# Gated linear attention and two MLPs: the scores of a chunk only within its halves, the first half handed to the second through the state

## The chip, the cores and the metric

One core of a Trainium2 chip. The time is the device time of one launch in microseconds (us), the median of three runs. TensorE (PE in the rows) multiplies matrices, VectorE (DVE), ScalarE (ACT) and GpSimd (POOL) work element by element, and SyncE (SP) issues the DMAs.

## The reference

Attention runs per head over 4 batches of 8 heads, 768 tokens, 48 features, and two MLPs follow:

```python
state = np.zeros((B, H, D, D)); y = np.zeros_like(q)
for t in range(S):
    state = alpha[:, :, t, :, None] * state + np.einsum('bhd,bhe->bhde', k[:, :, t], v[:, :, t])
    y[:, :, t] = np.einsum('bhd,bhde->bhe', q[:, :, t], state)
x = y.transpose(0, 2, 1, 3).reshape(B * S, H * D)   # 3072 tokens x 384
h = x @ w_in;  g = h * sigmoid(1.702 * h);  x = g @ w_out      # 384 -> 2048 -> 384
h = x @ w2_in; g = h - tanh(h);             out = g @ w2_out
```

The decay alpha is one number per token and feature, between 0.8 and 1.

## The kernel before

**Attention in chunks.** The 3072 tokens are cut into 24 chunks of 128, six to a sequence. All eight heads of a chunk are worked on together as four pairs: the features of a pair's first head lie on partitions 0 to 47, those of its second on 64 to 111. A chunk goes like this. Its decays are loaded twice, once reversed in time (L229), and two scans on VectorE (L237) turn them into running products; k and q are multiplied by these (`a_scale`), so that the decay between any two tokens of a chunk is a product of two factors. `a_scores` multiplies k with q: the keys are the stationary operand, 128 of them on 128 columns of the array, and 176 columns stream, 128 queries and then an identity of 48 that `eye` has written behind them, which gives k transposed for later. The two heads of a pair use the two row halves of the array. Call this group S (L273). It is done in two calls of two pairs each, x = 0 and x = 1. The scores leave PSUM under a causal mask: for the first eight chunks ScalarE copies and GpSimd cuts the triangle (L278, L283), for the others VectorE multiplies by a stored mask (L280, four instructions of 128x256 a chunk). ScalarE copies the transposed keys (L286).

`a_out` has three groups. Y (L302) multiplies the state that the earlier chunks left with q, 48 rows and 128 columns; the first chunk of a sequence has none. I (L305) multiplies the values with the masked scores, 128 rows and 128 columns, onto the same sums. D (L312) multiplies transposed keys with values, which is what the chunk adds to the state; the last chunk of a sequence has none. VectorE then adds it (L316) and multiplies by the decay of the chunk (L317). All of it is fp32, which the array does in two passes, and the trace counts each pass: eight matmuls are "x16".

`a_evac` copies the sums to SBUF (L326), sends them to DRAM and reads them back in the layout of the MLP (L331, L332), casts them to a high part (L333) and subtracts it to get a low part (L334).

**MLPs.** Each runs in six blocks of 512 tokens (j) and sixteen steps of 128 hidden units (m), 192 steps in all. A step has nine matmuls of 128x512 into the hidden layer (L343) and, three steps later, nine out of it (L350): three products of high and low parts for each of three pieces of the model dimension. Call these the MLP matmuls; there are 3456. Their activations and splits are on ScalarE, VectorE and GpSimd.

**Order.** The first four chunks come before the first MLP step, with the weights of the first MLP being converted on VectorE beside them (`conv`: L160, L161, L173, L191). The other twenty are spread over the steps of layer 1's first five blocks: `attend(g, r)`, r = 0 to 3, is called after the first matmuls of some steps. At r = 0 stand the first scan of the next chunk and the scores x = 0, at r = 1 the scores x = 1 and the second scan, at r = 2 `a_out` and the scaling of the next chunk, at r = 3 the evacuation and the loads of the chunk after the next. A scheduler that runs a model of the machine then decides the order of each engine's instructions, so groups are moved and broken up by it. DMAs are issued in order by SyncE.

Of the kernel before, what the change touches and what calls it, by code (L numbers as in the profile page):

```python
# [17 lines left out]
C = 128  # L18
# [13 lines left out]
CE = C + D  # L32
QW = 2 * AW + NP * C + NP * CE
# [35 lines left out]
def linear_attention_mlps(ctx, tc, xq, xv, fa, fv, cst, w1, w2, out):  # L69
# [13 lines left out]
    wt = [T(f"wt{i}", (128, WC), mybir.dt.int16) for i in range(2)]  # L83
# [16 lines left out]
    AR = 7184  # L100
# [15 lines left out]
    COLS = (AW, AW, NP * CE, NP * C, VW)  # L116
# [9 lines left out]
    third = [gt[:, 0:AW], gt[:, AW : 2 * AW], xsf[:, 0 : NP * CE], xsf[:, NP * CE :][:, :NB], gt[:, 2 * AW : 2 * AW + VW]]  # L126
    sm = [carve(4 * C) for _ in range(2)]
    kts = [carve(4 * D) for _ in range(2)]
# [36 lines left out]
    def w_check(l, m):  # L165
        t = wt[m % 2]
# [41 lines left out]

    def qq(g):
        return dec3(g, 2)  # L210
# [4 lines left out]
    def eye(g):  # L215
        for hh in range(2):
            r = slice(64 * hh, 64 * hh + D)
            A.copy(qq(g)[r, :, C:], ident[r, r].unsqueeze(1).to_broadcast([D, NP, D]))
# [4 lines left out]
    def a_load(g):  # L223
# [7 lines left out]
        SP.dma_start(out=qq(g)[:, :, :C], in_=xq[g, :, 2 * AW : 2 * AW + NB].rearrange("p (h t) -> p h t", h=NP))  # L231
# [9 lines left out]
    def a_scale(g):  # L241
        e = V if g < FULL else G
        e.tensor_tensor(out=qkk(g), in0=qkk(g), in1=dec3(g, 0)[:, :, :C], op=ALU.mult)  # L243
        e.tensor_tensor(out=qq(g)[:, :, :C], in0=qq(g)[:, :, :C], in1=dec3(g, 1)[:, :, 1:], op=ALU.mult)
# [21 lines left out]
    def a_scores(g, x, b):  # L266
        u = (2 * g + x) % 2
        q, k = qq(g), qkk(g)
        o = [bank[b + hh][:, : 2 * CE].rearrange("p (a t) -> p a t", a=2) for hh in range(2)]
        for i in range(2):  # L270
            for hh in range(2):
                r = slice(64 * hh, 64 * hh + D)
                P.matmul(out=o[hh][:, i], lhsT=k[r, 2 * x + i], rhs=q[r, 2 * x + i], start=True, stop=True)  # L273
        s4 = sm[u].rearrange("p (b a t) -> p b a t", b=2, a=2)
        kt = kts[u].rearrange("p (b a t) -> p b a t", b=2, a=2)
        for hh in range(2):
            if g < FULL:
                A.copy(s4[:, hh], o[hh][:, :, :C])  # L278
            else:
                V.tensor_tensor(out=s4[:, hh], in0=o[hh][:, :, :C], in1=mask.unsqueeze(1).to_broadcast([128, 2, C]), op=ALU.mult)  # L280
        if g < FULL:
            s3 = sm[u].rearrange("p (a t) -> p a t", a=4)
            G.affine_select(out=s3, in_=s3, pattern=[[0, 4], [1, C]], channel_multiplier=1, base=1 - C,  # L283
# [364 lines left out]
```

## Time and profile before

| | |
|---|---|
| median of three runs | 974.35 us (973.78 to 976.83) |
| the profiled execution | 975.3 us |
| its span | 973.2 us |
| mean granted clock of TensorE | 0.995 |
| TensorE busy | 940.9 us (97%) |
| VectorE, ScalarE, GpSimd busy | 606.0, 460.6, 191.7 us |

The rows below come from that execution; times in them start with its span. A matmul's duration in a row is longer than its share of TensorE's time, because matmuls overlap: what one costs is read from one start to the next. In a timeline row, the time is that of the first of the merged instructions, the duration runs to the end of the last, and the brackets hold the engine's idle time before it and what it waited for. `out<-in` are the program's names, `48*128 48x176` a weight of 48 rows and 128 columns and 48 rows of 176 streamed columns.

### The profile page before, as it was taken

The page shows a single profiled execution, that of the slowest core. Times are in us where ns is not written, and L with a number is a line of the kernel's source. Part 1 is how long each engine was busy: PE and PEld are TensorE (multiplying, and loading weights), DVE is VectorE, ACT ScalarE, POOL GpSimd, SP SyncE. Part 2 cuts the span into 40 slices and gives each one's busy share as a digit, 9 for nine tenths or more (in the row PEclk, how much of TensorE's full clock was granted, in tenths as well). Part 3 has the DMA queues.
Part 4 walks back from the last instruction along what each step waited for, and adds up shares of the span by engine and source line. Part 5 has one row for each costly group of instructions (what it writes and reads, how often), then busy time and mean ns, then how long its engine had stood idle before and what let it go on. Part 6 is the DMA issues. An engine that isn't in the chain of part 4 may idle for free.

```text
span 973.2 us, 13227 instructions
## 1 busy us (share of the span) xinstructions
PE 940.9 (97%) x4870; PEld 739.7 (76%) x4870; DVE 606.0 (62%) x914; ACT 460.6 (47%) x969; POOL 191.7 (20%) x150
## 2 busy tenths in 40 slices
PE   5968999999999999999999999999999999999997
PEld 4646787777777777777788888888888888888885
DVE  7989742442343453453339996766777777766663
ACT  4445434333443534434344555554556656545542
POOL 1222202434434434334230110100100101000000
PEclk9999999999999999999999999999999999999999
DMA  9795221432445463761324330100233420000001
GB/s 282 245 305 166 85 53 28 131 92 67 137 141 153 151 205 116 247 196 41 92 71 158 134 130 1 65 33 0 70 126 98 161 100 0 33 1 1 33 0 37
DMA packets 58043, 101.84 MB, mean 105 GB/s; under 512 B 4992, under 2 KB 37376, under 8 KB 57968
## 3 DMA queue, kind: packets, MB, share of 16 engines
q1 hardware_dynamic: 57968, 100.90, 32.6%
q8 instruction: 40, 0.66, 0.3%
q14 instruction: 35, 0.29, 0.1%
HBM read 86.73 MB, written 14.16 MB: 104 GB/s over the span
## 4 chain that ended last, share of the span: by engine, by line
PE 87%; DMA 5%; DVE 5%; issue 1%; ACT 1%; SPq 0%; POOL 0%; DVEq 0%; ACTq 0%
PE bank L350 40%; PE bank L343 40%; DMA arena<-xq 4%; PE bank L273 3%; PE bank L305 2%; DMA raw<-w 2%; DVE arena L237 1%; PE bank L302 1%; PE bank L312 1%; DVE cf L161 1%; DVE cf L173 1%; DVE wlo L191 0%; DVE cf L160 0%; DVE xs L173 0%; ACT arena L248 0%
## 5 line engine op out<-in xcount | busy, mean ns | idle before, releaser
L343 PE MATMUL bank<-xhi,whi 128*128 128x512 f32 x576 | 230.0, 400 | 0.2 <-ACT xhi L333 0.2
L343 PE MATMUL bank<-xlo,whi 128*128 128x512 f32 x576 | 229.8, 399 | 0.0
L343 PE MATMUL bank<-xhi,wlo 128*128 128x512 f32 x576 | 229.0, 398 | 0.0
L350 PE MATMUL bank<-ghi,whi 128*128 128x512 f32 x576 | 229.0, 398 | 0.0
L350 PE MATMUL bank<-ghi,wlo 128*128 128x512 f32 x576 | 228.5, 397 | 0.0
L350 PE MATMUL bank<-glo,whi 128*128 128x512 f32 x576 | 223.8, 396 | 0.0
L361 ACT CAST ghi<-gt 128x512 fp32r<-128x512 f32 x192 | 119.0, 620 | 199.2 <-DVE gt L373 124.1
L358 DVE SCALAR_TENSOR_TENSOR gt<-gt,bank 128x512 f32<-128x512 f32 x96 | 65.5, 682 | 125.8 <-ACT gt L357 122.7
L362 DVE TENSOR_TENSOR glo<-gt,ghi 128x512 fp32r<-128x512 f32 x128 | 93.2, 728 | 79.4 <-ACT ghi L361 76.0
L343 PEld LDWEIGHTS bank<-xhi,whi 128*128 128x128 f32 x576 | 109.0, 189 | 27.4 <-issue 1.6
L343 PEld LDWEIGHTS bank<-xlo,whi 128*128 128x128 f32 x576 | 109.1, 189 | 26.2 <-issue 1.4
L343 PEld LDWEIGHTS bank<-xhi,wlo 128*128 128x128 f32 x576 | 109.2, 190 | 25.7 <-issue 0.6
L350 PEld LDWEIGHTS bank<-ghi,whi 128*128 128x128 f32 x576 | 108.5, 188 | 26.4 <-issue 1.2
L350 PEld LDWEIGHTS bank<-ghi,wlo 128*128 128x128 f32 x576 | 108.5, 188 | 25.4 <-issue 0.8
L350 PEld LDWEIGHTS bank<-glo,whi 128*128 128x128 f32 x576 | 108.3, 188 | 25.1 <-DVE arena L243 0.2
L362 POOL TENSOR_TENSOR glo<-gt,ghi 128x512 fp32r<-128x512 f32 x64 | 85.8, 1341 | 139.0 <-ACT ghi L361 127.8
L410 POOL TENSOR_TENSOR xlo<-arena,xhi 128x512 fp32r<-128x512 f32 x18 | 27.9, 1574 | 307.6 <-ACT xhi L409 307.6
L357 ACT ACTIVATE gt<-bank 128x512 f32<-128x512 f32 x96 | 57.1, 595 | 64.0 <-PE bank L343 63.1
L237 DVE TENSOR_TENSOR_SCAN arena<-arena,seg 112x516 f32<-112x516 f32 x46 | 62.8, 1365 | 35.4 <-DMA arena<-xq 34.7
L371 DVE SCALAR_TENSOR_TENSOR arena<-arena,bank 128x512 f32<-128x512 f32 x96 | 65.7, 685 | 30.4 <-ACT arena L369 29.7
L369 ACT ACTIVATE arena<-bank 128x512 f32<-128x512 f32 x96 | 57.3, 597 | 42.2 <-PE bank L343 41.9
L373 DVE SCALAR_TENSOR_TENSOR gt<-arena 128x512 f32<-128x512 f32 x96 | 68.3, 711 | 9.4
(85 smaller groups left out, 853.7 us busy)
## 6 DMA issues: line engine op xcount, KB each, us to landing
raw<-w SPq DMA_DIRECT2D x64, 768.0 KB, 4.7
arena<-xq SPq DMA_DIRECT2D x46, 224.0 KB, 3.0
arena<-xq SPq DMA_DIRECT2D x22, 451.5 KB, 5.8
xt<-arena SPq DMA_DIRECT2D x96, 48.0 KB, 3.0
xlo<-xt SPq DMA_DIRECT2D x24, 192.0 KB, 4.1
x1t<-xs SPq DMA_DIRECT2D x6, 768.0 KB, 5.2
arena<-x1t SPq DMA_DIRECT2D x6, 768.0 KB, 4.6
out<-xs SPq DMA_DIRECT2D x18, 256.0 KB, 2.3
```

Of the source, the lines that this page charges most:

```text
L237: V.tensor_tensor_scan(out=dec(g, n), data0=src(g, n), data1=seg, initial=0.0, op0=ALU.mult, op1=ALU.max)
L273: P.matmul(out=o[hh][:, i], lhsT=k[r, 2 * x + i], rhs=q[r, 2 * x + i], start=True, stop=True)
L343: P.matmul(out=h, lhsT=w[m][:, ws], rhs=x[:, k, :n], start=c == 0, stop=c == 3 * KT - 1)
L350: P.matmul(out=acc[k][:, :n], lhsT=w[m][:, ws], rhs=x[s % 3][:, :n], start=m == 0 and c == 0, stop=m == MT - 1 and c == 2)
L357: A.activation(out=th[i][:, :n], in_=h, func=AF.Tanh, scale=0.851)
L358: V.scalar_tensor_tensor(out=gf[i][:, :n], in0=th[i][:, :n], scalar=1.0, in1=h, op0=ALU.add, op1=ALU.mult)
L361: A.copy(ghi[s % 3][:, :n], gf[s % 2][:, :n])
L362: e.tensor_tensor(out=glo[s % 3][:, :n], in0=gf[s % 2][:, :n], in1=ghi[s % 3][:, :n].bitcast(F32), op=ALU.subtract)
L369: A.activation(out=u, in_=h, func=AF.Square, accum_out=usum[:, s - NS1 :][:, :1])
L371: V.scalar_tensor_tensor(out=p, in0=u, scalar=P3, in1=h, op0=ALU.mult, op1=ALU.mult)
L373: V.scalar_tensor_tensor(out=gf[i], in0=w, scalar=PD, in1=p, op0=ALU.add, op1=ALU.mult)
L410: G.tensor_tensor(out=xlo[i][:, k], in0=xr[:, k], in1=xhi[i][:, k].bitcast(F32), op=ALU.subtract)
```

## The change

The chunk is treated as two halves of 64 tokens. Keys and values are stored reversed in time, so half u = 1 (partitions 64 to 127) is the first in time.

Scores are computed only within a half: sixteen matmuls of 64 keys, streaming 64 queries and the identity of 48 (112 columns), where there were eight of 128 keys and 176 columns. The two halves go to the two column halves of the array and the two heads to the two row halves, so four such tiles exist. One call makes all four pairs, into two banks. The mask is VectorE's for all chunks, two multiplications of 128x512 whose input is read twice along the queries; the quadrant of the mask that pairs first-half keys with second-half queries is set to zero. GpSimd's and ScalarE's part in the masking is gone. ScalarE copies the transposed keys as before, in two instructions.

`a_out` becomes two functions. `a_half`, at r = 1, makes D of the first half (eight matmuls over 64 keys), all of I (unchanged: 128 keys, with zeros in the quadrant), Y of the first half's queries (64 columns), then VectorE adds the first half's D to the state, or copies it for the first chunk of a sequence, and D of the second half is made. `a_rest`, at r = 2, makes Y of the second half's queries with the state so far, and the state gets the second D and the decay.

The queries are loaded by two DMAs, one a half, with shorter runs, since an identity now stands behind each half. The buffers of the masked scores and the transposed keys hold a whole chunk, once; the check of the second layer's weights has one buffer instead of two.

```diff
-CE = C + D
-QW = 2 * AW + NP * C + NP * CE
+
+C2 = C // 2
+CE = C2 + D
+QW = 2 * AW + NP * C + 2 * NP * CE
...
-    wt = [T(f"wt{i}", (128, WC), mybir.dt.int16) for i in range(2)]
+    wt = [T(f"wt{i}", (128, WC), mybir.dt.int16) for i in range(1)]
...
-    sm = [carve(4 * C) for _ in range(2)]
-    kts = [carve(4 * D) for _ in range(2)]
+    sm = carve(2 * NP * C).rearrange("p (b a t) -> p b a t", b=2, a=NP)
+    kts = carve(2 * NP * D).rearrange("p (b a t) -> p b a t", b=2, a=NP)
...
+    def qx(g):
+        return src(g, 2).rearrange("p (h x t) -> p h x t", h=NP, x=2)
+
     def qq(g):
-        return dec3(g, 2)
+        return qx(g)[:, :, :, :C2]
...
-        SP.dma_start(out=qq(g)[:, :, :C], in_=xq[g, :, 2 * AW : 2 * AW + NB].rearrange("p (h t) -> p h t", h=NP))
+        for x in range(2):
+            SP.dma_start(out=qq(g)[:, :, x], in_=xq[g, :, 2 * AW : 2 * AW + NB].rearrange("p (h x t) -> p h x t", h=NP, x=2)[:, :, x])
...
-    def a_scores(g, x, b):
-        u = (2 * g + x) % 2
-        q, k = qq(g), qkk(g)
-        o = [bank[b + hh][:, : 2 * CE].rearrange("p (a t) -> p a t", a=2) for hh in range(2)]
-        for i in range(2):
+    def a_scores(g, b):
+        q, k = qx(g), qkk(g)
+        o = [bank[b + hh][:, : NP * CE].rearrange("p (a t) -> p a t", a=NP) for hh in range(2)]
+        for p in range(NP):
+            for hh in range(2):
+                for u in range(2):
+                    r, st = slice(64 * hh, 64 * hh + D), slice(C2 * u, C2 * u + C2)
+                    P.matmul(out=o[hh][st, p], lhsT=k[r, p, st], rhs=q[r, p, 1 - u], start=True, stop=True)
+        for hh in range(2):
+            A.copy(kts[:, hh], o[hh][:, :, C2:])
+        for hh in range(2):
+            V.tensor_tensor(out=sm[:, hh].rearrange("p a (x t) -> p a x t", x=2),
+                            in0=o[hh][:, :, :C2].unsqueeze(2).to_broadcast([128, NP, 2, C2]),
+                            in1=mask.rearrange("p (x t) -> p x t", x=2).unsqueeze(1).to_broadcast([128, NP, 2, C2]), op=ALU.mult)
+
+
+    def y_at(b, p, hh, u):
+        return bank[b + hh][64 * (p % 2) : 64 * (p % 2) + D, C * (p // 2) + C2 * (1 - u) :][:, :C2]
+
+    def y_state(g, b, u):
+        for p in range(NP):
             for hh in range(2):
                 r = slice(64 * hh, 64 * hh + D)
...
+                P.matmul(out=y_at(b, p, hh, u), lhsT=state[r, p], rhs=qq(g)[r, p, 1 - u], start=False, stop=not u and p >= 2)
+
+    def deltas(g, u):
+        dl = bank[7][:DP, NP * D * u : NP * D * (u + 1)].rearrange("p (a e) -> p a e", a=NP)
+        st = slice(C2 * u, C2 * u + C2)
+        for p in range(NP):
+            for hh in range(2):
+                P.matmul(out=dl[64 * hh : 64 * hh + D, p], lhsT=kts[st, hh, p], rhs=vt(g)[st, p, D * hh : D * hh + D],
+                         start=True, stop=True)
+        return dl
+
+    def a_half(g, b):
         c = g % NCH
...
+        dl = deltas(g, 1)
+        for p, hh in [(p, hh) for x in range(2) for hh in range(2) for p in (2 * x, 2 * x + 1)]:
+            P.matmul(out=bank[b + hh][64 * (p % 2) : 64 * (p % 2) + D, C * (p // 2) :][:, :C], lhsT=vt(g)[:, p, D * hh : D * hh + D],
+                     rhs=sm[:, hh, p], start=p < 2, stop=False)
         if c:
...
+            y_state(g, b, 1)
+            V.tensor_tensor(out=state, in0=dl, in1=state, op=ALU.add)
+        else:
+            V.tensor_copy(state, dl)
         if c < NCH - 1:
+            deltas(g, 0)
+
+    def a_rest(g, b):
+        y_state(g, b, 0)
+        if g % NCH < NCH - 1:
             dl = bank[7][:DP, : NP * D].rearrange("p (a e) -> p a e", a=NP)
...
+            V.tensor_tensor(out=state, in0=dl, in1=state, op=ALU.add)
+            V.tensor_tensor(out=state, in0=state, in1=dec3(g + 1, 0)[:, :, C:].to_broadcast([DP, NP, D]), op=ALU.mult)
...
-    def attend(g, r, b0=5, b1=5):
+    def attend(g, r, b=5):
         if r == 0:
             prep(g + 1, 0)
-        if r < 2:
-            a_scores(g, r, (b0, b1)[r])
+            a_scores(g, b)
+        if r == 1:
+            a_half(g, b)
         if r == 2:
-            a_out(g, b0)
+            a_rest(g, b)
...
+    V.memset(mask[C2:, C2:], 0.0)
```

How the change moves instructions shows at three places. The first is TensorE in the middle of layer 1 (a chunk's output groups; the names are the lines of each kernel). Before:

```order
L302 MATMUL bank_129<-arena,state 48x128
L302 MATMUL bank_130<-arena,state 48x128
L305 MATMUL bank_129<-arena 48x128 x2
L305 MATMUL bank_130<-arena 48x128 x2
L305 MATMUL bank_129<-arena 48x128 x2
L305 MATMUL bank_130<-arena 48x128 x2
L312 MATMUL bank_131<-arena 48x48 x4
```

And now, where a chunk's middle stands:

```order
L303 MATMUL bank_130<-arena 48x48 x8
L311 MATMUL bank_128<-arena 48x128 x2
L311 MATMUL bank_129<-arena 48x128 x2
L311 MATMUL bank_128<-arena 48x128 x2
L311 MATMUL bank_129<-arena 48x128 x2
L296 MATMUL bank_128<-arena,state 48x64
L296 MATMUL bank_129<-arena,state 48x64
```

Y stood ahead of I and D behind it; now D of the first half leads, I follows, and Y comes last, with D of the second half (not in the piece) behind it.

The second is VectorE in the same stretch of the program, between scores and state: scans (L237, now L243), masks (L280, now L284) and an MLP instruction (L358, now L365). Before:

```order
L358 SCALAR_TENSOR_TENSOR gt<-gt,bank_127 128x512
L237 SCALAR_TENSOR_TENSOR arena<-arena,seg 112x516
L239 RECIPROCAL seg<-arena 112x4
L280 TENSOR_TENSOR arena<-bank_129,cs 128x256
L237 SCALAR_TENSOR_TENSOR arena<-arena,seg 112x516
L236 MEMSET seg 112x4
L280 TENSOR_TENSOR arena<-bank_130,cs 128x256
```

And now:

```order
L243 SCALAR_TENSOR_TENSOR arena<-arena,seg 112x516
L245 RECIPROCAL seg<-arena 112x4
L243 SCALAR_TENSOR_TENSOR arena<-arena,seg 112x516
L242 MEMSET seg 112x4
L284 TENSOR_TENSOR arena<-bank_128,cs 128x512
L284 TENSOR_TENSOR arena<-bank_129,cs 128x512
L365 SCALAR_TENSOR_TENSOR gt<-gt,bank_127 128x512
L315 TENSOR_TENSOR state<-bank_130,state 112x192
```

One pair of masks stood between the two scans of the next chunk and one behind both; now both masks stand behind both scans, and the addition in mid-chunk (L315) follows them.

The third is VectorE before the first MLP matmul, behind the subtraction that makes chunk 2's low part (L334, now L341), with scans and weight conversions of the fourth chunk's time. Before:

```order
L334 TENSOR_TENSOR xlo_106<-xlo_106,xhi_104 128x3x128
L316 TENSOR_TENSOR state<-bank_131,state 112x192
L237 SCALAR_TENSOR_TENSOR arena<-arena,seg 112x516
L191 TENSOR_TENSOR wlo_87<-xs,whi_71 128x768
L173 SCALAR_TENSOR_TENSOR cf_102<-raw_95,cf_102 128x768
L317 TENSOR_TENSOR state<-state,arena 112x192
```

And now:

```order
L341 TENSOR_TENSOR xlo_105<-xlo_105,xhi_103 128x3x128
L243 SCALAR_TENSOR_TENSOR arena<-arena,seg 112x516
L162 TENSOR_SCALAR xs<-raw_97 128x768
L315 TENSOR_TENSOR state<-bank_130,state 112x192
L193 TENSOR_TENSOR wlo_83<-xs,whi_67 128x768
L245 RECIPROCAL seg<-arena 112x4
L249 TENSOR_TENSOR arena<-arena 112x512
L163 SCALAR_TENSOR_TENSOR xs<-raw_97,xs 128x768
L162 TENSOR_SCALAR cf_101<-raw_95 128x768
L243 SCALAR_TENSOR_TENSOR arena<-arena,seg 112x516
L284 TENSOR_TENSOR arena<-bank_128,cs 128x512
L284 TENSOR_TENSOR arena<-bank_129,cs 128x512
L325 TENSOR_TENSOR state<-bank_130,state 112x192
```

Before, the subtraction and then the state's addition (L316) and decay (L317) of a chunk came in close order; now the addition in mid-chunk (L315), two masks (L284) and the addition of the second half (L325) all stand behind that subtraction.

## Rows read from the trace of the kernel before

**Rows 1.** The page, part 1: busy time and share of the span, by engine.

```profile
PE 940.9 (97%) x4870; PEld 739.7 (76%) x4870; DVE 606.0 (62%) x914; ACT 460.6 (47%) x969; POOL 191.7 (20%) x150
```

**Rows 2.** Windows: length; PE, PEld, DVE, ACT, POOL busy (count); clock, DMA share, GB/s.

```profile
0.00:66.00 66.00, 46.83 (x305) 34.84 (x306) 57.79 (x86) 29.66 (x80) 14.20 (x14) 1.00 0.90 275
66.00:112.00 46.00, 41.67 (x212) 29.56 (x211) 44.19 (x66) 22.79 (x50) 10.59 (x6) 0.93 0.52 159
112.00:480.00 368.00, 366.23 (x2262) 281.99 (x2261) 155.09 (x264) 149.94 (x334) 134.24 (x108) 1.00 0.40 122
480.00:966.00 486.00, 486.00 (x2096) 393.33 (x2094) 348.23 (x500) 257.37 (x505) 32.65 (x22) 1.00 0.19 63
```

**Rows 3.** The page, part 4: the chain of waits that ended last, by engine.

```profile
PE 87%; DMA 5%; DVE 5%; issue 1%; ACT 1%; SPq 0%; POOL 0%; DVEq 0%; ACTq 0%
```

**Rows 4.** Timeline of TensorE from its first MLP matmul, waits in brackets.

```profile
65.50 1.03 PE L343 MATMUL bank<-xhi,whi 128*128 128x512 f32 x2 [0.18 <-ACT xhi L333]
...
68.11 0.87 PE L273 MATMUL bank<-arena 48*128 48x176 f32 x8 [1.58 <-ACT whi L190]
...
78.00 0.64 PE L302 MATMUL bank<-arena,state 48*48 48x128 f32 x8 [2.75 <-ACT arena L286]
```

**Rows 5.** Timeline of TensorE, 300 to 309 us: start, duration, operation, number merged.

```profile
300.30 0.40 PE L343 MATMUL bank<-xlo,whi 128*128 128x512 f32 x1
300.63 0.87 PE L273 MATMUL bank<-arena 48*128 48x176 f32 x8
301.43 0.38 PE L312 MATMUL bank<-arena 128*48 128x48 f32 x8
301.75 0.50 PE L343 MATMUL bank<-xhi,wlo 128*128 128x512 f32 x1
302.08 0.40 PE L343 MATMUL bank<-xhi,whi 128*128 128x512 f32 x1
...
306.04 0.40 PE L343 MATMUL bank<-xhi,wlo 128*128 128x512 f32 x1
306.37 0.66 PE L302 MATMUL bank<-arena,state 48*48 48x128 f32 x16
306.95 1.08 PE L305 MATMUL bank<-arena 128*48 128x128 f32 x16
307.87 0.35 PE L312 MATMUL bank<-arena 128*48 128x48 f32 x8
308.14 0.51 PE L343 MATMUL bank<-xhi,whi 128*128 128x512 f32 x1
308.49 0.39 PE L343 MATMUL bank<-xlo,whi 128*128 128x512 f32 x1
```

**Rows 6.** Timeline of TensorE at 347 us: a scores group broken in two.

```profile
347.04 0.86 PE L273 MATMUL bank<-arena 48*128 48x176 f32 x4
347.83 0.51 PE L343 MATMUL bank<-xhi,whi 128*128 128x512 f32 x1
...
348.74 0.86 PE L273 MATMUL bank<-arena 48*128 48x176 f32 x4
```

**Rows 7.** Groups of instructions by line, VectorE: busy us, mean ns, idle before.

```profile
L280 DVE TENSOR_TENSOR arena<-bank,cs 128x256 f32<-128x256 f32 x64 | 24.2, 415 | 18.4 <-PE bank L273 18.3
L316 DVE TENSOR_TENSOR state<-bank,state 112x192 f32<-112x192 f32 x16 | 5.7, 353 | 16.3 <-PE bank L312 16.2
L358 DVE SCALAR_TENSOR_TENSOR gt<-gt,bank 128x512 f32<-128x512 f32 x96 | 65.5, 682 | 125.8 <-ACT gt L357 122.7 <-POOL arena L244 2.8
```

**Rows 8.** The decay loads, line 229, 140 to 480 us: issue to landing.

```profile
DMA to landing us min/median/max: 3.9/6.0/9.6
```

**Rows 9.** Who waited for whom, TensorE, 140 to 480 us: total, times, longest.

```profile
PE bank L302 <- ACT arena L286: 1.4, 2, 0.8
```

**Rows 10.** Timeline of ScalarE at 56 us: cast of chunk 2, copy of chunk 3.

```profile
55.60 0.51 ACT L333 CAST xhi<-xlo 128x384 fp32r<-128x384 f32 x1 [2.51 <-DMA xlo<-xt]
56.02 0.64 ACT L326 COPY arena<-bank 112x256 f32<-112x256 f32 x2
```

More of the change, by code (lines that the diff above doesn't have):

```diff
@@ L217, in eye @@
             r = slice(64 * hh, 64 * hh + D)
-            A.copy(qq(g)[r, :, C:], ident[r, r].unsqueeze(1).to_broadcast([D, NP, D]))
+            A.copy(qx(g)[r, :, :, C2:], ident[r, r].unsqueeze(1).unsqueeze(1).to_broadcast([D, NP, 2, D]))
     def vt(g):
@@ L243, in a_scale @@
         e.tensor_tensor(out=qkk(g), in0=qkk(g), in1=dec3(g, 0)[:, :, :C], op=ALU.mult)
[L244 removed]
+        e.tensor_tensor(out=qq(g), in0=qq(g), in1=dec3(g, 1)[:, :, 1:].rearrange("p h (x t) -> p h x t", x=2), op=ALU.mult)
     def a_guard(g):
@@ L276, in a_scores @@
[L276 to L283, printed above, removed]
-                            compare_op=ALU.is_ge, fill=0.0)
@@ L285, in a_scores @@
-        for hh in range(2):
-            A.copy(kt[:, hh], o[hh][:, :, C:])
-    def a_out(g, b):
-        c = g % NCH
-        q = qq(g)
-        y = [bank[b + hh][:, : 2 * C].rearrange("p (a t) -> p a t", a=2) for hh in range(2)]
-        heads = [(p, hh) for a in range(2) for hh in range(2) for p in (2 * a, 2 * a + 1)]
-        def at(p, hh):
-            return y[hh][64 * (p % 2) : 64 * (p % 2) + D, p // 2]
-        if c:
-            for p in range(NP):
-                for hh in range(2):
-                    r = slice(64 * hh, 64 * hh + D)
-                    P.matmul(out=at(p, hh), lhsT=state[r, p], rhs=q[r, p, :C], start=p < 2, stop=False)
-        for p, hh in heads:
-            s4 = sm[p // 2].rearrange("p (b a t) -> p b a t", b=2, a=2)
-            P.matmul(out=at(p, hh), lhsT=vt(g)[:, p, D * hh : D * hh + D], rhs=s4[:, hh, p % 2],
-                     start=not c and p < 2, stop=p >= 2)
+                P.matmul(out=y_at(b, p, hh, u), lhsT=state[r, p], rhs=qq(g)[r, p, 1 - u], start=False, stop=not u and p >= 2)
@@ L307, in a_out @@
         if c < NCH - 1:
+            deltas(g, 0)
+    def a_rest(g, b):
+        y_state(g, b, 0)
+        if g % NCH < NCH - 1:
             dl = bank[7][:DP, : NP * D].rearrange("p (a e) -> p a e", a=NP)
-            for p in range(NP):
-                for hh in range(2):
-                    kt = kts[p // 2].rearrange("p (b a d) -> p b a d", b=2, a=2)
-                    P.matmul(out=dl[64 * hh : 64 * hh + D, p], lhsT=kt[:, hh, p % 2], rhs=vt(g)[:, p, D * hh : D * hh + D],
-                             start=True, stop=True)
@@ L314, in a_out @@
-            al = dec3(g + 1, 0)[:, :, C:].to_broadcast([DP, NP, D])
-            if c:
-                V.tensor_tensor(out=state, in0=dl, in1=state, op=ALU.add)
-                V.tensor_tensor(out=state, in0=state, in1=al, op=ALU.mult)
-            else:
-                V.tensor_tensor(out=state, in0=dl, in1=al, op=ALU.mult)
+            V.tensor_tensor(out=state, in0=dl, in1=state, op=ALU.add)
+            V.tensor_tensor(out=state, in0=state, in1=dec3(g + 1, 0)[:, :, C:].to_broadcast([DP, NP, D]), op=ALU.mult)
```

15 lines of the change are left out of this document (6 added, 9 removed).

## The prediction

> **What bounds the kernel now.** I read the busy shares first, then the span by windows, then the chain, then TensorE's timeline. TensorE is busy 97% of the span [rows 1]. By windows it is 366.23 of 368 us from 112 to 480 and all of the 486 us behind that, and only 46.83 of the first 66 [rows 2]: there DMA (0.90 busy) and VectorE (57.79 of 66) stand beside it. The chain gives TensorE 87%, and 5% each to DMA and VectorE [rows 3], which are the start. So two things can move the time: what the attention groups take on TensorE between the MLP matmuls, and when the first MLP matmul starts, at 65.50 us [rows 4]. The MLP work is unchanged: 486.00 us with 2096 matmuls is 0.232 us each [rows 2], 3456 of them 802 us.
>
> **How a group is priced.** A matmul's own duration is too long a measure; I take starts. In the timeline of a chunk [rows 5] the MLP matmul at 300.30 is followed by another 1.78 us later, with S and D between that and 302.08; one MLP matmul stands between, so two steps of 0.23 come off: S and D together cost 1.32. From 306.04 to 308.49 it is 2.45 less 0.46: Y, I and D cost 1.99. D alone is 301.43 to 301.75, 0.32, behind S, and 307.87 to 308.14, 0.27, behind I; without it S costs 1.00. A usual chunk has one S alone, one S with D, and one Y with I and D: 1.00 + 1.32 + 1.98 = 4.30 us.
>
> The pieces: S takes 0.80 (300.63 to 301.43) for 8 passes of 176 columns, two abreast; Y 0.58 for 16 passes of 128, four abreast; I 0.92 for 16 passes of 128, two abreast; D 0.27 to 0.32 for 8 passes of 48, two abreast [rows 5]. With 0.83 ns a column (two cycles at the granted 2.4 GHz, an estimate) the streaming is 0.59, 0.43, 0.85 and 0.16, and rests of 0.07 to 0.21 are left for filling and for the switch from one tile shape to the next. Entering a group costs 0.10 (300.30 to 300.63, less 0.23), leaving it about 0.11 (308.14 to 308.49, less 0.23).
>
> **The change on TensorE.** S now has 32 passes of 112 columns. Four abreast that is 8 x 112 x 0.83 = 0.75, with a rest of 0.17 and entry and exit 1.13 us, once a chunk. Four abreast is what Y shows today, 16 passes in 0.58 us. The middle group has D of one half (16 passes, 0.32 + 0.1), I (0.85 + 0.13), Y of one half (16 passes of 64 columns, four abreast, 0.21 + 0.12) and entry, exit and switches: about 2.07. The last group has Y of the other half and D of the other half, 0.33 + 0.42 + 0.2: 0.95. The sum is 4.15, so 0.15 less a chunk; the rests alone make that -0.3 to 0. One group a chunk goes, D doubles (half the keys each, but as many columns to stream), Y is halved twice, S loses a quarter.
>
> Of chunks 7 to 23, twelve are usual (-1.8 us); two open a sequence and gain a Y of the second half (+0.08 each); three close one and come out even. Together -1.6 us, from -3.4 to +0.2.
>
> The scheduler breaks groups. Before, five S of these chunks are cut by MLP matmuls. In the worst way, as at 347 us, four passes take 0.79 us, as long as eight otherwise (347.04 to 347.83), since the two heads no longer run abreast, and the second four come later [rows 6]: 1.0 us more. Two are like this, and three that keep the heads together cost some 0.4: 3.2 us. In the new order I count four breaks, at about 0.35: 1.4. That is -1.8 us, from -3.2 (no break costs) to 0. For chunks 5 and 6, ahead of 112 us, I take the same 0.15 each and one bad break: -1.0, with bounds of -2 and 0.
>
> **Masks, copies, state.** VectorE masked a chunk in four steps of 415 ns [rows 7]; two of 128x512 take at most the 682 ns that an MLP step of that size from PSUM takes [rows 7], 1.36 for 1.66. The extra state addition is 353 ns [rows 7]. In the middle VectorE is busy 155.09 of 368 us [rows 2], so this is hidden; GpSimd's and ScalarE's lost masking (up to chunk 8) is hidden too and worth nothing by itself. What can show is the order. Both masks stand behind both scans of the next chunk in seven chunks, and the scans wait for the decay load, which lands 3.9 us at the least, 6.0 in the median and 9.6 at the most after its issue [rows 8]. From the issue, just behind the last group, I count about 40 MLP matmuls (9.3 us), S and D of the next chunk (1.6) to the point at which I needs the masks: 10.9 us. Two scans and two masks take some 3.8 of it before and 2 in slack for the issue, so the load has about 4.9 us. Half the loads are later than that; yet the places of issue and need move with the order, and TensorE's largest wait for ScalarE there is now 1.4 us in the whole stretch [rows 9]. I take 2 us as before, so no term, bounded by 0 and +33 (seven chunks of 9.6 - 4.9).
>
> **The start.** Here VectorE gets ten masks (about 6 us) and four additions (1.1) more ahead of the first MLP matmul, and the order lets two weights slip behind it (about 4.8 less). The weights are far ahead of their use, so the sum itself matters little; the place does. Today the copy of chunk 3's sums follows chunk 2's cast by 0.42 us on ScalarE (55.60 to 56.02) [rows 10], and that cast waited 2.51 us for the trip of chunk 2 through DRAM. Now chunk 3's addition in mid-chunk stands on VectorE behind chunk 2's subtraction, which waits for the same trip, with a scan and a weight conversion between; only then can Y of the second half, and the copy, follow. Subtraction 0.5, scan 1.3, conversion 0.5, addition 0.35, Y 0.3: about 2.9 for 0.42, so the first MLP matmul slips by 2.5 us. Against that TensorE waits 1.58 and 2.75 us soon behind its first MLP matmuls, for ScalarE [rows 4]; what it waits for doesn't hang on that matmul, so part of it is eaten by the slip. I take 1.5. The term is +1.0, with bounds of -4.3 (no slip, both waits go) and +5.0 (the slip comes at chunk 2 as well, and nothing is given back). The queries' loads in shorter runs add to a DMA that is busy 0.90 there [rows 2]; they are in that upper bound.
>
> **Sum.** -1.6 - 1.8 - 1.0 + 1.0 = -3.4. The profiled execution took 975.3, 0.95 above the median 974.35: 971.9 there, 971.0 on the median. What a measurement of this kernel can tell from no change is about 0.3%, 2.9 us: below 971.4 is faster, above 977.3 slower.
>
> **The rivals.** (1) The start gets better: the groups in front of it need fewer instructions on ScalarE and none on GpSimd, and the later waits go. -4.3 in place of +1.0: 965.7. For it speaks that 4.3 us of wait stand there [rows 4]; against it the order on VectorE.
>
> (2) The start slips whole, +5.0: 975.0. For it speaks the wait of 2.51 us on the DRAM trip [rows 10].
>
> (3) The slower side: the masks wait for decays. I, and with it every MLP matmul behind it, waits for two masks queued behind a scan whose load hasn't landed. At the median landing of 6.0 it is 1.1 us, with what the longer ones add some 1.9 a chunk, in seven chunks 13: 984. It decides where a load lands later than 4.9 us after its issue. For it: the median of 6.0 [rows 8]; against it: only 1.4 us of such waits today [rows 9], and before one pair of masks was behind a scan as well.
>
> (4) The passes of Y are too short for their rate. Sixteen passes four abreast in 0.21 us would start every 13 ns. The nearest row has 8 passes of D in 0.27 us [rows 5], 25 ns each with the smallest rest of 0.07 taken off; no row shows 13. If passes can't start closer than D's do, Y of a half costs 0.40 twice where 0.21 stood, some 0.38 a chunk in 19 chunks, +7: 978. Against it: four abreast, Y's 16 passes have 0.43 for streaming today, 27 ns each [rows 5], which is what their columns need and so shows no floor. The Trainium skill has a floor of this kind (TensorE: Matmul & The Clock Gate, section "Wait — 56ns, not 53.3ns?"): from one matmul's start to the next it is never below about 25 ns, however few the columns. By that rule this rival would be the outcome; no run here shows passes short enough to test it.
>
> (5) It doesn't do what it says: the tiles of S run only two abreast, since the order puts eight passes of one bank behind eight of the other in some chunks. Then S costs 0.75 more, in 17 chunks +13: 984.
>
> **Chances.** The forecast 0.45 (own range 967 to 975), rival 1 0.16, rival 2 0.13, rival 3 0.13, rival 4 0.07, rival 5 0.06. Faster by over 0.3%: 0.27 of the forecast and rival 1, 0.43. Within: 0.18 and 0.08 of rival 2, 0.26. Slower: 0.31, from rivals 3 to 5 and the rest of 2. The range of 962 to 982 leaves out the best of rival 1 and most of rivals 3 and 5.
>
> **What would show it.** In the profile of the changed kernel: S as one group with 1.1 us between MLP matmuls (rival 5: 1.9); Y of a half 0.3 us long (rival 4: 0.5); the three groups of a chunk together 4.0 to 4.3; the first MLP matmul at 66 to 70 us, and less than 3 us of waits behind it to 112; waits of I for the masks on VectorE below 3 us between 112 and 480 (rival 3: over 8). The forecast is wrong if the part from 112 on is not shorter by 2 to 5 us, or if the start moves by more than 5.

## The result and the profile after

The changed kernel took 981.8 us (median of six runs; one of them, at a granted clock of 0.672, took 1308 us and stands outside the ratio) against 974.98 of the kernel before; the ratio is 1.0059 with a 95% interval of 1.0033 to 1.0085. Run again in a later job it was 1.0047 (1.0024 to 1.0071). I had predicted 971.0: the time rose where I had it fall. The profiled execution has a span of 979.9 us, 6.7 more than before.

The page's busy line and its chain, to be held against [rows 1] and [rows 3]:

```profile
PE 930.7 (95%) x6022; PEld 735.1 (75%) x6022; DVE 613.1 (63%) x927; ACT 447.3 (46%) x889; POOL 172.7 (18%) x134
PE 81%; DMA 9%; DVE 6%; issue 1%; ACT 1%; SPq 1%; DVEq 0%; ACTq 0%
```

TensorE is busy for 10 us less and ends 7 later; its share of the chain fell from 87% to 81%, and DMA's rose from 5% to 9%. So its busy time shrank and the waiting grew by more. The windows say where, with the columns of [rows 2]:

```profile
0.00:66.00 66.00, 33.55 (x480) 26.64 (x480) 54.59 (x92) 20.22 (x42) 0.20 (x4) 1.00 0.82 237
66.00:112.00 46.00, 41.45 (x309) 30.24 (x306) 42.27 (x66) 20.45 (x39) 0.00 (x0) 0.96 0.68 203
112.00:480.00 368.00, 362.63 (x3102) 279.55 (x3101) 167.64 (x270) 145.50 (x299) 136.14 (x106) 0.99 0.42 125
480.00:973.00 493.00, 493.00 (x2139) 398.68 (x2137) 348.06 (x501) 260.39 (x509) 36.32 (x24) 1.00 0.18 61
```

In the middle TensorE is idle for 5.4 us of 368 where it was 1.8. In the first 66 us it is busy for 33.55 us in place of 46.83, with two Ys and both D of chunk 4 still to come, and yet the first MLP matmul comes at 68.64, not 65.50. Two timelines show the middle. First a chunk's three groups, as in [rows 5]:

```profile
295.65 0.39 PE L357 MATMUL bank<-ghi,whi 128*128 128x512 f32 x1
295.97 1.00 PE L280 MATMUL bank<-arena 48*64 48x112 f32 x32
296.90 0.50 PE L357 MATMUL bank<-ghi,wlo 128*128 128x512 f32 x1
297.24 0.39 PE L357 MATMUL bank<-glo,whi 128*128 128x512 f32 x1
...
301.66 0.40 PE L357 MATMUL bank<-ghi,whi 128*128 128x512 f32 x1
301.99 0.56 PE L303 MATMUL bank<-arena 64*48 64x48 f32 x16
302.48 1.08 PE L311 MATMUL bank<-arena 128*48 128x128 f32 x16
303.49 0.44 PE L296 MATMUL bank<-arena,state 48*48 48x64 f32 x16
303.86 0.50 PE L357 MATMUL bank<-ghi,wlo 128*128 128x512 f32 x1
304.20 0.39 PE L357 MATMUL bank<-glo,whi 128*128 128x512 f32 x1
...
308.62 0.40 PE L357 MATMUL bank<-ghi,whi 128*128 128x512 f32 x1
308.95 0.51 PE L303 MATMUL bank<-arena 64*48 64x48 f32 x13
...
309.67 0.51 PE L357 MATMUL bank<-ghi,wlo 128*128 128x512 f32 x1
310.01 0.39 PE L357 MATMUL bank<-glo,whi 128*128 128x512 f32 x1
```

The scores are one group: 0.93 us from 295.97 to 296.90 for 32 passes, so four abreast. With entry and exit they take 297.24 - 295.65 - 0.46 = 1.13 us, the middle group 304.20 - 301.66 - 0.46 = 2.08, and the last 310.01 - 308.62 - 0.46 = 0.93: 4.14 where 4.30 stood. Then the stretch at the start of the fifth block:

```profile
407.60 0.99 PE L280 MATMUL bank<-arena 48*64 48x112 f32 x30
411.04 0.79 PE L350 MATMUL bank<-xhi,whi 128*128 128x512 f32 x1 [2.44 <-ACT xhi L340]
...
412.91 0.63 PE L357 MATMUL bank<-ghi,wlo 128*128 128x512 f32 x1
413.34 0.63 PE L357 MATMUL bank<-glo,whi 128*128 128x512 f32 x1
...
417.95 0.39 PE L350 MATMUL bank<-xlo,whi 128*128 128x512 f32 x1
```

TensorE waits 2.44 us for the cast of chunk 19, and behind it the MLP matmuls start 0.43 us apart (412.91 to 413.34) instead of 0.23: a window from 412.5 to 417.5, in the columns above, has the granted clock at 0.50, that is 1.2 GHz.

```profile
412.50:417.50 5.00, 5.00 (x12) 3.94 (x13) 4.93 (x7) 1.40 (x5) 1.36 (x1) 0.50 0.68 220
```

Twelve matmuls pay 0.195 each, 2.3 us. What else TensorE waited for, from 112 to 480 us, stands here in the columns of [rows 9]:

```profile
PE bank L350 <- ACT xhi L340: 3.0, 2, 2.4
PE bank L311 <- DVE seg L242: 1.2, 3, 0.9
PE bank L311 <- DVE arena L284: 1.2, 3, 0.6
```

I waits for VectorE: for masks (L284), or for the scan's small step in front of them (L242). And the start, first on VectorE, then on ScalarE (the place of [rows 10]):

```profile
55.87 0.56 DVE L341 TENSOR_TENSOR xlo<-xlo,xhi 128x384 fp32r<-128x384 f32 x1 [0.46 <-ACT xhi L340]
57.72 1.23 DVE L243 TENSOR_TENSOR_SCAN arena<-arena,seg 112x516 f32<-112x516 f32 x1 [1.29 <-DMA arena<-xq]
58.87 0.53 DVE L162 TENSOR_SCALAR xs<-raw 128x768 int32<-128x768 int32 x1
59.32 0.35 DVE L315 TENSOR_TENSOR state<-bank,state 112x192 f32<-112x192 f32 x1
```

```profile
55.33 0.51 ACT L340 CAST xhi<-xlo 128x384 fp32r<-128x384 f32 x1 [0.90 <-DMA xlo<-xt]
55.74 0.83 ACT L192 CAST whi<-xs 128x768 fp32r<-128x768 f32 x1
60.69 0.54 ACT L282 COPY arena<-bank 128x192 f32<-128x192 f32 x2 [4.12 <-PE bank L303]
61.14 0.84 ACT L333 COPY arena<-bank 112x256 f32<-112x256 f32 x2
```

The chain that I had named is there, subtraction, scan, conversion, addition, Y, copy, with a wait of 1.29 for chunk 5's decays in it: the copy of chunk 3 comes 5.81 us behind chunk 2's cast, where it was 0.42 and I had counted 2.9.

### The profile page after: what moved, and what is told of

Read it like the earlier page. It is cut to its first block, busy times and chain, and to the rows that moved or that the text cites. A ratio compares the mean times of both kernels' runs of the same rounds, so it can differ in the third digit from the quotient of the medians.

```text
span 979.9 us, 15497 instructions
## 1 busy us (share of the span) xinstructions
PE 930.7 (95%) x6022; PEld 735.1 (75%) x6022; DVE 613.1 (63%) x927; ACT 447.3 (46%) x889; POOL 172.7 (18%) x134
## 4 chain that ended last, share of the span: by engine, by line
PE 81%; DMA 9%; DVE 6%; issue 1%; ACT 1%; SPq 1%; DVEq 0%; ACTq 0%
PE bank L350 38%; PE bank L357 37%; DMA arena<-xq 4%; DMA raw<-w 2%; DMA xlo<-xt 2%; PE bank L311 2%; DVE arena L243 2%; PE bank L303 2%; PE bank L280 1%; PE bank L296 1%; DVE arena L284 1%; DVE cf L163 1%; DMA xt<-arena 0%; SPq L338 0%; DVE wlo L193 0%
## 5 line engine op out<-in xcount | busy, mean ns | idle before, releaser
L365 DVE SCALAR_TENSOR_TENSOR gt<-gt,bank 128x512 f32<-128x512 f32 x96 | 65.4, 681 | 123.1 <-ACT gt L364 122.7
L243 DVE TENSOR_TENSOR_SCAN arena<-arena,seg 112x516 f32<-112x516 f32 x46 | 61.7, 1340 | 44.3 <-DMA arena<-xq 43.5
```

Source lines behind the costliest of these rows:

```text
L243: V.tensor_tensor_scan(out=dec(g, n), data0=src(g, n), data1=seg, initial=0.0, op0=ALU.mult, op1=ALU.max)
L365: V.scalar_tensor_tensor(out=gf[i][:, :n], in0=th[i][:, :n], scalar=1.0, in1=h, op0=ALU.add, op1=ALU.mult)
```

## The experiments

All were timed in five rounds against the kernel before. The table has what I read first in each profile: the start of chunk 3's copy on ScalarE and of the first MLP matmul, and the time from the first to the last MLP matmul. The 3456 take 802.6 us by themselves; what is over that is the extra time of the expectations. The copy has two parts, and the start of the first is given.

| kernel | copy of chunk 3 | first MLP matmul | first to last | ratio to before |
|---|---|---|---|---|
| before | 56.0 | 65.5 | 900.3 | |
| changed | 61.1 | 68.6 | 904.0 | 1.0059 (1.0033 to 1.0085) |
| e1, changed again | 61.6 | 71.0 | 899.4 | 1.0047 (1.0024 to 1.0071) |
| e2, subtraction on GpSimd | 60.9 | 71.0 | 899.5 | 1.0044 (1.0016 to 1.0073) |
| e3, check's loads spread | 60.6 | 70.8 | 900.9 | 1.0021 (0.9998 to 1.0044) |
| e4, before with short runs of q | 52.7 | 65.9 | 901.1 | 0.9964 (0.9938 to 0.9989) |
| e5, before with VectorE's masks | 49.8 | 62.5 | 903.6 | 0.9999 (0.9981 to 1.0018) |
| e6, masks back, first 8 chunks | 61.9 | 72.3 | 905.0 | 1.0103 (1.0068 to 1.0139) |
| e7, scans behind masks | 62.8 | 71.8 | 894.3 | 1.0003 (0.9983 to 1.0022) |
| e8, weights held | 61.1 | 70.3 | 899.1 | 1.0025 (1.0009 to 1.0041) |
| e9, early scans behind additions | 59.1 | 69.4 | 904.1 | 1.0051 (1.0030 to 1.0073) |
| e10, e9 and e2 | 59.1 | 68.8 | 898.4 | 1.0011 (0.9989 to 1.0032) |
| e11, scans behind masks from chunk 7 | 62.8 | 70.1 | 898.8 | 0.9985 (0.9968 to 1.0002) |
| e12, e10 and e11 | 59.1 | 69.4 | 890.4 | 0.9955 (0.9939 to 0.9970) |
| e13, nothing passed on | 57.6 | 67.9 | 918.8 | 1.0229 (1.0203 to 1.0256) |
| e14, e12 with weights held | 58.1 | 67.9 | 892.8 | 0.9930 (0.9913 to 0.9948) |
| e15, before with late scans | 55.0 | 65.4 | 898.8 | 0.9989 (0.9978 to 1.0000) |

**Does it come back, and is it the DMAs?** e1 is the changed kernel, unedited.

> The changed kernel itself, once more, to see which of its stalls come back. Theory A: the loss has two places. At the start chunk 3's addition in mid-chunk stands on VectorE behind chunk 2's trip through DRAM, a scan and a weight conversion: first MLP matmul again at 68 to 69 us (65.5 before). At the fifth block chunk 19's trip takes 17 us, because weight loads stand among its DMAs: TensorE waits 2 to 3 us for the cast near 405 us and runs at half clock some 12 MLP matmuls behind it. Time 980 to 982. Rival B: that stall was one execution's chance; then it is missing here and the median is 975 to 978.

The late start came back, even later. Of the stall at the fifth block 0.7 us came back, and no slow stretch behind it; yet the median was 979.93, between the two theories. So the late start is the rule, and the size of the stall differs from run to run.

e2, the subtraction off VectorE:

```diff
-        (V if g < FULL else G).tensor_tensor(out=xl[:, :, o], ...
+        G.tensor_tensor(out=xl[:, :, o], ...
```

> The changed kernel with the low part's subtraction of the first eight chunks on GpSimd, which has 0.2 us of work in the first 66, so that VectorE's queue no longer stands behind the DRAM trip. Theory A: chunk 3's copy starts 2 to 4 us behind chunk 2's cast (5.8 now), the first MLP matmul at 65.5 to 67, the time 2 to 3 us under the changed kernel's of the same job. Rival C (the queries' 256-byte runs slow the DMAs at the start): the first MLP matmul stays at 68 to 69 and the time is the changed kernel's within 1 us.

Nothing moved (71.0, 979.7 us). The addition of chunk 3 still started at 59.1, behind the scan of chunk 5.

e3, the loads for the weight check:

```diff
-            if 2 <= j < 4 and m % 2:
-                w_check(l, 8 * (j - 2) + m // 2)
...
+            j0, n8 = (1, 4) if l == 1 else (2, 8)
+            if j0 <= j < j0 + 16 // n8 and m < 2 * n8:
...
```

> The changed kernel with the 16 weight loads of layer 1's check spread over the first halves of blocks 1 to 4 (four each) in place of all steps of blocks 2 and 3, so that none stands at a block's end. Theory A: chunk 19's low-part load lands 3 to 6 us after its issue (10.2 now), TensorE doesn't wait for its cast, the clock stays at 1.00 there, and the time is 5 to 6 us under the changed kernel's: 975 to 977. Rival C: the loads of q are as slow as before, the change is under 1 us. Rival B (chance): under 1.5 us against the changed kernel of the same job.

The low-part load of chunk 19, issue to landing, first of the changed kernel, then of e1, then of e3:

```profile
DMA to landing us min/median/max: 10.2/10.2/10.2
```

```profile
DMA to landing us min/median/max: 8.8/8.8/8.8
```

```profile
DMA to landing us min/median/max: 2.4/2.4/2.4
```

With no weight loads beside it, the load lands in 2.4 us and TensorE doesn't wait for that cast. The time is 3.4 us under e1 by the medians and 2.5 by the ratios (1.0021 and 1.0047), but the two intervals overlap, and in e3's profile I waits 5.1 us for VectorE, where it is 3.8 in e1: the stall is shown to go, the gain in time is not. The 5 to 6 us expected were priced from the changed kernel's first profile, in which this stall was larger than in e1.

e4 puts one part into the kernel before: q in two DMAs with runs of 256 bytes.

```diff
-        SP.dma_start(out=qq(g)[:, :, :C], in_=...)
+        for x in range(2):
+            SP.dma_start(out=qq(g)[:, :, C // 2 * x : C // 2 * (x + 1)], in_=...[:, :, x])
```

> The kernel before with one part of the change alone: q is loaded by two DMAs a chunk with runs of 256 bytes. Theory A: these DMAs have slack nearly everywhere; first MLP matmul at 65 to 67, time within 1 us of the kernel before. Rival C: 3 to 6 us slower than before, with the first MLP matmul 3 us later.

The start stayed at 65.9 and the time fell by 0.36%: the short runs cost the kernel no time. Why it was faster I did not find out.

**Is it VectorE's amount of work?** e5, the first eight chunks masked by VectorE in the kernel before (`if g < FULL` and its copies and cut removed):

> The kernel before with one part of the change alone: the masks of the first eight chunks on VectorE (four of 128x256 a chunk) in place of ScalarE and GpSimd. So far the first MLP matmul stands at 65.5 and 65.9 us in the kernel before and its variant with short runs, at 68.6 to 71.0 in the changed kernel and two variants of it. Theory F (VectorE, busy nearly all the time ahead of the first MLP matmul, sets the start, and the masks, additions and conversions in its one queue delay each chunk): the first MLP matmul at 67.5 to 70, time 2 to 4 us over the kernel before. Rival G (the passing on in mid-chunk is the delay: D, addition, Y, in a row for every chunk): 65 to 66.5, time within 1 us of before.

e6, the reverse in the changed kernel:

```diff
+            if g < FULL:
+                for x in range(2):
+                    st = slice(C2 * x, C2 * x + C2)
+                    A.copy(sm[st, hh, :, C2 * (1 - x) : C2 * (1 - x) + C2], o[hh][st, :, :C2])
+                continue
...
+                G.affine_select(out=s, in_=s, pattern=[[0, 2 * NP], [1, C2]], ...
```

> The changed kernel with the masks of the first eight chunks back on ScalarE and GpSimd (four copies of 64x256 and two triangle cuts of 64x512 a chunk). Theory F: the first MLP matmul at 66 to 68 us, time 2 to 4 us under the changed kernel. Rival G: it stays at 68.5 to 71, time within 1 us of the changed kernel. Past 120 us nothing differs by either.

e8, the conversions of all but the first weights queued behind chunk 3's low part:

```diff
-                conv(1)
+                if m < 2:
+                    conv(1)
+                else:
+                    with tc.issue_after(low[3].ins):
+                        conv(1)
```

> The changed kernel with all weight conversions on VectorE but those of the first three weights (and parts of two more) queued behind chunk 3's low part: 17 conversion steps in place of 33 stand ahead of it, some 13 us less for VectorE. Theory F: the first MLP matmul at 62 to 66 us; the time falls by 3 to 6 us if the weights still come in time, by less if MLP matmuls then wait for their low parts. Rival H (the trip through DRAM and the loads set 12 to 13 us a chunk whatever VectorE does): the first MLP matmul stays at 68 to 71.

The first MLP matmuls of e5, e6 and e8:

```profile
62.54 1.22 PE L336 MATMUL bank<-xhi,whi 128*128 128x512 f32 x2
```

```profile
72.31 1.22 PE L360 MATMUL bank<-xhi,whi 128*128 128x512 f32 x2
```

```profile
70.33 1.22 PE L352 MATMUL bank<-xhi,whi 128*128 128x512 f32 x2 [3.17 <-ACT xhi L342]
```

With more masks on VectorE the first MLP matmul came 3 us earlier; masks taken off it, or 13 us of conversions, did not bring it back. By this mark theory F is out: in the changed kernel with the weights held the addition of chunk 3 stood at 59.3 as ever, behind the scan. But e5 and e6 lie outside the ranges of both theories, and e6 was slower than the changed kernel (1.0103). The mark is also uneven: in e5 the first MLP matmul stands ahead of I and Y of chunk 4, which it followed before, and the time stayed the same (0.9999). The last part comes back to that.

**Is it the order on VectorE?** e7 queues both scans of the next chunk behind this chunk's masks:

```diff
-            prep(g + 1, 0)
             a_scores(g, b)
+            with tc.issue_after(last[g].ins):
+                prep(g + 1, 0)
```

> The changed kernel with both scans of the next chunk queued on VectorE behind the masks of this one, so that no mask and no addition of a chunk stands behind a scan that waits for a decay load. TensorE's waits of I for VectorE between 112 and 480 us, 2.4 to 5.1 us in the changed kernel's profiles, fall under 1 us by the theory that masks wait for decays; by the rival that they wait because VectorE is busy they stay at 2 to 5. At the start chunk 3's copy comes 3 to 4.5 us behind chunk 2's cast (5.8 to 6.5 now) by theory F. Time 2 to 4 us under the changed kernel if both hold, within 1 us if neither.

Two profiles' waits of TensorE from 130 to 480 us, first e1 (the changed kernel), then e7:

```profile
PE bank L311 <- DVE arena L284: 2.4, 6, 1.2
PE bank L311 <- DVE seg L242: 1.4, 3, 1.0
PE bank L350 <- ACT xhi L340: 0.7, 1, 0.7
```

```profile
PE bank L305 <- DVE state L319: 1.1, 1, 1.1
PE bank L352 <- ACT xhi L342: 1.1, 1, 1.1
PE bank L313 <- DVE seg L242: 0.2, 1, 0.2
```

I's waits for VectorE fell from 3.8 to 0.2 us, and the time by 4.3 against e1 (0.44% by the ratios). The start did not gain: with its scans later, chunk 4's came too late. e9 therefore treats the start apart: for the first seven chunks a scan goes behind the mid-chunk addition two chunks earlier (`queued` is `tc.issue_after` around `prep`).

```diff
+            added[g] = V.tensor_tensor(out=state, in0=dl, in1=state, op=ALU.add)
...
+            if g < 7:
+                queued(added.get(g - 1), g + 1, 0)
```

> The changed kernel with, for the first seven chunks, the scans of a chunk queued on VectorE behind the mid-chunk addition two chunks earlier. Less VectorE work ahead of the first MLP matmul, or masks elsewhere, did not bring it forward (70.3 and 72.3 us), so theory F is out. Theory J: chunk 3's addition (59.3 in four profiles) waits in the queue for the scan of chunk 5 and its decay load, issued at 53.3, and the copy, the trip and the first MLP matmul wait for the addition. By J the addition moves to 54 to 57 us, the copy of chunk 3 to 57 to 59, the first MLP matmul to 65 to 68, and the time falls by 2 to 4 us. Rival H (the trips set the pace, whatever VectorE's order): 68.5 to 71, time within 1 us of the changed kernel.

e10 is e9 with e2's edit, e11 the order of e7 from chunk 7 on alone, e12 all three.

> As the one with scans behind additions, and the first eight chunks' low parts on GpSimd besides, so that the addition of chunk 3 stands behind no transfer at all. By J the addition at 53 to 55 us, the copy right behind chunk 2's cast (55 to 57), the first MLP matmul at 63.5 to 66.5, the time 3 to 5 us under the changed kernel. By H no change.

> The changed kernel with scans queued behind the masks only from chunk 7 on; the start as in the changed kernel. With all scans so, the extra time between MLP matmuls fell from 96.8 to 91.7 us in the profiles, and the start came later. By the theory that masks wait behind scans for decay loads: extra time 91 to 93, no wait of I over 0.3 us past 130 us, first MLP matmul as in the changed kernel (68.5 to 71), time 4 to 5 us under the changed kernel, about that of the kernel before. If the first chunks' order gave the gain: extra time 95 to 97 and no gain.

> All three together: scans behind additions for the first seven chunks, behind masks from there on, low parts on GpSimd. If the two causes are the whole of the loss and add up: first MLP matmul at 63.5 to 66.5, extra time 91 to 94, the last MLP matmul at 959 to 963, the time 968 to 971, that is 3 to 6 us under the kernel before. If the start's cause is another: 973 to 976.

Chunk 3's addition came forward by 2 us only, as this piece of VectorE's timeline of e12 shows:

```profile
52.96 1.81 DVE L175 SCALAR_TENSOR_TENSOR xs<-raw,xs 128x768 int32<-128x768 int32 x2
54.80 2.52 DVE L193 TENSOR_TENSOR wlo<-xs,whi 128x768 fp32r<-128x768 f32 x2
57.24 0.34 DVE L317 TENSOR_TENSOR state<-bank,state 112x192 f32<-112x192 f32 x1
58.00 1.23 DVE L243 TENSOR_TENSOR_SCAN arena<-arena,seg 112x516 f32<-112x516 f32 x1
```

With the scan gone from in front of it, two weights' conversions stood there. By the start theory J missed; e9 alone gained nothing (980.6), e10 3.5 us against e1 by the ratios. e11 gained 6.0, though its profiled execution, 977.9 where its median is 973.8, shows little of it: I waits 0.2 us, as expected, but the extra time is 96.2, in the other theory's range. There D waits 1.6 us and a cast costs 1.1, and behind these two waits seven and eight MLP matmuls start 0.43 us apart. All three together beat the kernel before by 0.45%. Against e1 that is 0.92%, about the sum of e10 (0.36) and e11 (0.62), so the two add up. The time of e12 (970.2) and its last MLP matmul (959.8) came in their ranges, but not as expected: the first MLP matmul missed its range by 3 us, and the extra time, 87.8 against 91 to 94, made up for it.

**Does the passing on delay the start at all?** In e13 the mid-chunk addition goes to a spare tile, so what a first half passes on is left out:

```diff
-            V.tensor_tensor(out=state, in0=dl, in1=state, op=ALU.add)
+            V.tensor_tensor(out=spare, in0=dl, in1=spare, op=ALU.add)
```

> The changed kernel, but the first half's share is added to a spare tile in mid-chunk instead of to the state (so what the first half passes to the second and to later chunks is left out); all instructions stay, only nothing waits for that addition. Theory K: the start comes late because a chunk's copy now needs an addition of its own chunk, which stands in VectorE's queue behind whatever waits there (a scan that waits for its load, or, with that scan moved, two weight conversions). Then here the copy of chunk 3 follows chunk 2's cast by 1 to 3 us, and the first MLP matmul stands at 63 to 67 us. Rival H (trips and loads alone): 68.5 to 71.

Chunk 3's copy came 2.6 us behind chunk 2's cast, as theory K has it, but the first MLP matmul only at 67.9, outside both. Its total says nothing of this: D waited for the additions to the spare tile, up to 7.8 us at a time. e14 takes the last instructions from in front of the addition, in e12's order, by holding the weights back behind `added[3]`:

> As the run with all three together, and the weight conversions but those of the first three weights queued on VectorE behind chunk 3's mid-chunk addition, which in that run still stood at 57.2 us behind two conversions. Theory K: the addition at 53 to 55, the copy of chunk 3 at 55 to 57, the first MLP matmul at 63 to 67 (69.4 in that run), the time 2 to 5 us under it, 965 to 968, if the weights come in time. Rival H: first MLP matmul 68 to 71, time within 1 us of that run.

```profile
54.21 0.36 DVE L317 TENSOR_TENSOR state<-bank,state 112x192 f32<-112x192 f32 x1 [0.91 <-PE bank L298]
```

```profile
67.87 1.22 PE L352 MATMUL bank<-xhi,whi 128*128 128x512 f32 x2 [4.75 <-ACT xhi L342]
```

The addition now waits for TensorE alone and stands at 54.2, 5 us earlier than in the changed kernel. The copy came at 58.1 and not by 57, the first MLP matmul 1.5 us before e12's, again short of 63 to 67. At 967.47 us it is the fastest kernel here, 0.7% under the one before; the time is in its range, but what it gains over e12 (0.25% by the ratios) is hardly more than the noise.

e15, the late scans in the kernel before, from chunk 8 on:

> The kernel before with both scans queued behind both pairs of masks from chunk 8 on, to see what that order is worth without the change. Before has 2.9 us of waits that this can take away; by that the time is 1 to 3 us under the kernel before. If the queue matters only where both masks stand behind both scans, as in the changed kernel, under 1 us.

It gained 0.8 us by the medians, 1.1 by the ratio (interval 0 to 2.1), which lies at the line between the two. The order is worth less there than the 6.0 us of e11: it is the changed kernel, with both masks behind the scans, that needed it. The early orders and the subtraction on GpSimd were not tried in the kernel before, so what they are worth without the change is not known.

## Why the prediction was wrong

**The groups on TensorE: right.** Predicted 1.13, 2.07 and 0.95 us a chunk, measured 1.13, 2.08 and 0.93. Over chunks 7 to 23 that is -2.3 us (-1.6 predicted), and groups broken by MLP matmuls cost 1.4 where they had cost 3.6 (-2.2; -1.8 predicted). Rivals 4 and 5 are out: Y of a half takes 0.37 us to the next start (303.49 to 303.86), 23 ns a pass with switch and exit in it; in the trace the sixteen starts lie within 0.23 us, 15 ns apart. The Trainium skill's floor of about 25 ns from start to start (TensorE: Matmul & The Clock Gate, section "Wait — 56ns, not 53.3ns?") is not seen across four tiles. The Trainium skill's page TensorEngine Tiling (Array Packing), section "Key Properties", has tiles run their matmuls in parallel, and with that the trace agrees: 32 passes of 112 columns took 0.93 us, where at the prediction's 0.83 ns a column they would need 3.0 one after the other.

**The masks: the term I set to zero was not zero.** This is the step "I take 2 us as before, so no term". In the profile the waits and slow stretches of chunks 7 to 23 came to 10.6 us against 3.0. Some 3.5 are waits for masks, as rival 3 had them, at a quarter of its price; the decay loads landed in 4.7 us in the median (line 234, 140 to 480 us), where I had counted 6.0. The 1.4 us that I held against rival 3 [rows 9] were of another kind: there Y waits for ScalarE's copies, not I for masks. But 6.0 belong to a place that I had not looked at: chunk 19's trip, with a load of 10.2 us where it took 4.9, and the clock's fall behind the wait. A chunk's last group now comes mostly 6 to 8 us behind its middle; chunk 19's copy started at 393.4 us, 391.8 before, and its transfers fell among the weight loads. e3 takes the trip's stall away and e7 the waits for masks, which was worth 4.3 us; what e3's is worth in time is not clear of the noise.

**The start: the term mis-sized.** I had +1.0 (2.5 lost, 1.5 given back) and -1.0 for chunks 5 and 6. Measured are 3.1 at the first MLP matmul and 0.65 more to the end of chunk 6: 3.8 in place of 0.0. That is near rival 2's slip (+5.0, with the -1.0 for chunks 5 and 6: 4.0). The delay between cast and copy was 5.4 us longer, not 2.5, since the scan also waited for its decays. The waits of [rows 4] went, but others came. The four longest from 60 to 112 us are these:

```profile
PE bank L303 <- DVE state L315: 4.0, 1, 4.0
PE bank L311 <- DVE arena L284: 3.3, 1, 3.3
PE bank L350 <- ACT xhi L340: 1.6, 1, 1.6
PE bank L350 <- DVE xlo L341: 0.9, 1, 0.9
```

The first three end at 59.73, 64.32 and 68.64 us, so they stand ahead of the first MLP matmul: there TensorE waits for the addition in mid-chunk, for masks and for the cast. Behind it TensorE waits 3.0 us in all to 112 us, where it waited 4.3. So 1.3 came back, near the 1.5 that I had counted; but two Ys and a D of chunk 4, which had stood ahead of the first MLP matmul, now stand behind it, and by the end of chunk 6 nothing is left of the gain.

The sum, for the one profile: 3.8 - 2.3 - 2.2 + 7.6 = +6.9, against the 6.7 us of the spans. In e1's profile the loss is split otherwise: 4.6 us to the end of chunk 6, and nothing behind it, where waits of 4.8 us used up what the groups gain. So the start is what came back, and the stall at chunk 19's trip is the part that varies.

**What stays open.** In 13 of 17 profiles the first MLP matmul comes 9 to 10.4 us behind chunk 3's copy (7.3 to 13.2 in all), so the copy mostly sets it. Of the 5.1 us by which the copy was late, e9, e13 and e14 take back 2 to 3.5, all by what stands in front of the addition. The rest is there from the first chunks on (chunk 0 is copied at 23.2 us, 19.8 before). In the changed kernel the masks of chunk 0 stand behind a scan of chunk 1 that waits 1.9 us for its load; in e7, with scans behind masks, chunk 0 is copied at 19.9.

The first MLP matmul is a poor mark, since groups of chunk 4 can stand on either side of it. Take instead the first MLP matmul behind chunk 6's last group, less 0.232 us for each MLP matmul ahead of it: before, 107.21 - 95 x 0.232 = 85.2; changed, 123.77 - 150 x 0.232 = 89.0, which is the 3.8 of the sum. By this mark the start takes 87.9 to 91.6 us in e1, e2, e3, e6, e7 and e11, 86.4 in e9, and 83.3 to 84.7 in e8, e10, e12, e13 and e14. So three different edits each take the whole loss away, in one profile each: the weights held back (e8), scans and subtraction moved (e10), or nothing waiting for the addition (e13). All three leave VectorE less to do ahead of what others wait for; how much of the loss is the addition's place and how much the amount of work, which theory F had, was not separated. In e8 and e9 the time hardly fell, since the stretch behind chunk 6 was 4.1 and 6.4 us longer than in e1.

## What to carry to other kernels

Price a dependency that is put into the middle of a step by the queue that it lands in, not by its own instruction: the addition took 0.35 us, and it came 5 us later than in e14, where nothing stood in front of it; in the changed kernel a scan stood there, which waited for a load. When matmul time falls, look at what has been hidden by it: the transfers at the ends of blocks need their own slack. An order that a scheduler has found is worth pinning at such places: here the same matmuls lost 0.6% in one order and gained 0.7% in another, with one subtraction on another engine. The kernel before was given only one of these orders (e15), so how much of the 0.7% is the change's own is not known.

## What was not expected of the hardware

Short passes four abreast start faster than I had a row for: a whole group of 16 with 64 columns takes 0.37 us. A wait of 2.44 us was followed by twelve matmuls at 1.2 GHz, 2.3 us more; in e1, with a wait of 0.7 at the same place, none followed. The length of the wait alone doesn't tell: in e11 the granted clock was 0.50 and 0.53 behind waits of 1.64 and 1.11 us, and in e10 it stayed at 1.00 behind one of 1.95. Runs of 256 bytes instead of 512 on a load of 224 KB cost no time (e4, 0.9964), though each of the two halves landed 3.8 us after its issue in the median, where the whole load had taken 3.3.
